# Attention rows and router logits turned by one TensorE product with an identity, stored by one DMA a step

## The chip, the core and the metric

The kernel runs on one core of a Trainium2 chip. Its engines work at the same time and wait for one another through semaphores: PE is TensorE (matrix products; PEld is its weight load), DVE is VectorE, ACT is ScalarE, POOL is GpSimd, and SP is the engine whose only work here is to issue DMAs. Matrix products read SBUF and write PSUM, which has eight banks of 128 partitions x 512 f32. The metric is the device time of one execution in microseconds (us); less is better. The kernel before took 461.04 us, the median of 3 runs (459.53 to 462.3).

## The reference

Two stages, of which the second takes the first one's result as its rows:

```python
# attention: q, k, v are (B, H, S, D) = (4, 8, 768, 64), blocks of 64 positions
for b in range(nb):
    qb, kb, vb = (q[:, :, sl], k[:, :, sl], v[:, :, sl])
    intra = np.einsum('bhic,bhjc->bhij', qb, kb) * Dmask[None]
    intra = np.einsum('bhij,bhjd->bhid', intra, vb)
    inter = np.einsum('bhid,bhde->bhie', qb * lam_pow[None], kv_state)
    out[:, :, sl] = intra + inter
    kv_state = lam_block[None, :, None, None] * kv_state + np.einsum('bhsd,bhse->bhde', kb * rev_pow[None], vb)
x = attn_out.transpose(0, 2, 1, 3).reshape(B * S, H * D)       # 3072 rows of 512
# router and experts: E = 8, w1 (8, 512, 1024), w2 (8, 1024, 512)
logits = x @ w_gate
expert_idx = np.argmax(logits, axis=1)
gate_w = softmax(logits)[arange, expert_idx]
for e in range(E):
    xe = x[expert_idx == e]
    out[expert_idx == e] = gate_w[..., None] * (np.maximum(xe @ w1[e], 0.0) @ w2[e])
```

## The kernel before, in words

**Attention.** It goes through 12 steps, six blocks of 128 positions (`n`) by two pairs of batch entries (`b`); one step takes 8 heads of two batch entries. In the loop of line 933 and after, `cur` is the step whose attention is finished now, `ahead` the next one, whose q and k are turned and scored already, and `last` the one before, whose rows leave now. The iterations are called i = 0 to 11 below. PE, DVE, ACT and SP do their work in the order in which the program writes it; POOL's larger work is chained one by one (`in_line`).

An iteration does, in this order on PE: `logits(last)` (four products against `gate`, line 361), `turn_ahead` (16 PE transposes of q and k, lines 242 and 257, into banks 0 to 3), the sum of the logits (`sum_logits`, line 368), the product of q with the running state (line 309, banks 6 and 7), the new state's product (`grow`, line 343, bank 4), scores times v (line 321, banks 6 and 7), the other half of line 309, every second iteration the ranks of the tokens within their experts (line 423, bank 5), and the scores of `ahead` (line 285, banks 0 to 3). DVE multiplies the scores by the decay mask (`mt`, line 291), which frees banks 0 to 3; ACT copies q and k out of PSUM (`qT`, `kT`, lines 244 and 259).

The attention's result stands in PSUM as features x tokens (`m.op`, banks 6 and 7). It is wanted twice: as it stands, for the router's logits (`to_sbuf`, an ACT copy `xT`), and as rows of tokens in DRAM (`xs`). DVE makes the rows by two 32x32-block transposes of 128 x 512 a step (`to_rows`, line 335); they leave a tile `x` in which a partition holds 32-wide pieces of many tokens, so `store_rows` (line 375) writes them by four DMAs a step with runs of 512 bytes. In half of the feature chunks the two heads of a pair stand in swapped order (`out_at`, `u ^ (hp & 1)`), and the rows keep that order; so `load_first` (line 191) loads the first weights of every expert pass by three DMAs, two of which swap halves of 64 rows.

Once a group of steps is complete, `choose` finds each token's expert on DVE, `weigh` its weight, `put` (line 423 and after) its slot, and POOL scatters slot entries to DRAM by indirect DMAs (line 436). SP issues, in one queue, the stores of `last` and the loads of step i + 3 (line 109: three DMAs of 512 KB in runs of 256 bytes), then at the loop's end the weights of the first pass.

**Experts.** After the loop the tokens of expert 0 come first, those of the early steps in a first part (`0a`), the others after it (`0b`), then the seven other experts, their products by a Strassen-like scheme of seven for eight (lines 692, 714 and 790). The rows are gathered from `xs` by POOL's indirect DMAs (line 520).

## Time and profile before

| What | Value |
|---|---|
| median of the runs | 461.04 us |
| the profiled execution, its own time | 459.43 us |
| its span, first to last instruction | 457.1 us |
| around the span | 2.3 us |
| busy PE, DVE, ACT, POOL | 423.9, 286.2, 140.6, 119.1 us |
| granted TensorE clock, mean | 0.981 of full |
| DMA, mean over the span | 209 GB/s, 138256 packets |
| end of the attention on PE | 139.4 us |
| first product of the experts | 142.6 us |

Rows of an engine's timeline read: start in us, duration, engine, line, operation, output<-input, shapes, how many in a row, and in brackets how long the engine was idle before and what ended it. `SPq` is SP's queue; a DMA row there is the time SP needed to hand the DMA over, not the transfer. A chain row "DMA a<-b" is the time from that hand-over to the data's landing. A row of a stretch gives its length, each engine's busy time with its instructions, the clock that PE was granted (1.00 is full), the share of the 16 DMA engines' time that packets took (it can pass 1, packets overlap), and what they moved in GB/s.

### The profile page before, as it was taken

Reading aid. Unit: us, or ns where it says so; the run is one execution under the profiler, and the core shown is the slowest. Engines: PE = TensorE matmul, PEld = TensorE weight load, DVE = VectorE, ACT = ScalarE, POOL = GpSimd, SP = SyncE. Lnnn points to the kernel's source line nnn. Section 1 sums busy time; section 2 is a strip of 40 time slices with the busy share of each in tenths; the row PEclk is TensorE's granted clock in tenths of the full one; section 3 lists DMA queues with packets and bytes.
Section 4 is the critical chain, followed back from the end, with each engine's and each line's share of the span. In section 5 each row is a group of like instructions: output and inputs, shape, how many; then the busy total and the mean of one; then the engine's idle time right before and its main releaser. Section 6 shows DMA issues by size and latency. Waiting matters only on the chain.

```text
span 457.1 us, 8958 instructions
## 1 busy us (share of the span) xinstructions
PE 423.9 (93%) x3527; PEld 387.9 (85%) x3527; DVE 286.2 (63%) x585; ACT 140.6 (31%) x298; POOL 119.1 (26%) x135
## 2 busy tenths in 40 slices
PE   3989897988889999898999999999999999999993
PEld 3877776867767749898999999999999999999873
DVE  3859494959476105798288568739938938948311
ACT  3344242433223111143134313413513512512511
POOL 5425353536143054005110320420230110010022
PEclk9999899999898999999999999999999999999998
DMA  9999998999998799977997997996995994613212
GB/s 177 235 213 211 154 213 175 201 169 198 187 260 141 229 235 259 325 189 193 359 225 214 371 217 183 364 266 172 335 294 123 331 275 97 227 67 70 69 66 71
DMA packets 138256, 95.53 MB, mean 209 GB/s; under 512 B 82787, under 2 KB 117223, under 8 KB 138205
## 3 DMA queue, kind: packets, MB, share of 16 engines
q1 hardware_dynamic: 130861, 80.76, 72.9%
q0 software_dynamic: 5264, 13.58, 10.4%
q10 hardware_dynamic: 2080, 0.52, 0.6%
q8 instruction: 30, 0.49, 0.5%
q14 instruction: 21, 0.17, 0.1%
HBM read 70.41 MB, written 24.65 MB: 208 GB/s over the span
## 4 chain that ended last, share of the span: by engine, by line
PE 70%; DMA 13%; DVE 8%; SPq 5%; issue 2%; ACT 1%; POOLq 0%; POOL 0%; DVEq 0%; ACTq 0%
PE p L692 26%; PE p L714 23%; DMA k_in<-in_k_dram 7%; PE ph L569 5%; PE po L818 5%; DMA qkv_in<-in_k_dram 4%; SPq L109 3%; PE p L790 3%; PE op L321 2%; PE tk L257 2%; PE po L734 2%; DVE ohc L402 1%; SPq L375 1%; DVE mt L291 1%; DMA ye<-yb 1%
## 5 line engine op out<-in xcount | busy, mean ns | idle before, releaser
L526 POOL DMA_INDIRECT out_dram<-o,list x21 | 22.1, 1054 | 166.9 <-ACT o L778 162.7
L714 PE MATMUL p<-hT,w2t 128*128 128x204 f32 (+3 forms) x288 | 49.9, 330 | 0.0
L714 PEld LDWEIGHTS p<-hT,w2t 128*128 128x128 f32 x288 | 48.2, 190 | 0.0
L702 ACT ACTIVATE hT<-hT 128x408 f32<-128x408 f32 (+4 forms) x56 | 29.4, 527 | 50.7 <-DVE hT L701 50.5
L692 PE MATMUL p<-xgT,w1t 128*128 128x204 f32 (+4 forms) x224 | 39.2, 328 | 0.0
L520 POOL DMA_INDIRECT xg<-xs,list x24 | 24.8, 1033 | 52.7 <-DMA list<-slots 31.1
L722 DVE TENSOR_TENSOR yT<-p,u_qsT 128x408 f32<-128x408 f32 (+3 forms) x18 | 10.2, 568 | 44.7 <-ACT u_qsT L608 29.2
L692 PEld LDWEIGHTS p<-xgT,w1t 128*128 128x128 f32 x224 | 37.1, 190 | 0.2 <-DVE xgT L546 0.2
L701 DVE TENSOR_TENSOR hT<-p,u_qsT 128x408 f32<-128x408 f32 (+4 forms) x42 | 23.4, 561 | 17.2 <-PE p L692 12.4
L291 DVE TENSOR_TENSOR mt<-sp,decay 128x512 f32<-128x512 f32 x48 | 29.8, 682 | 5.7 <-PE sp L285 5.7
L436 POOL DMA_INDIRECT slots<-entry,slot_i x24 | 23.6, 983 | 26.7 <-DVE slot_i L434 13.3
L285 PEld LDWEIGHTS sp<-qT,kT 64*128 64x128 f32 x384 | 23.5, 195 | 4.1 <-issue 2.0
L285 PE MATMUL sp<-qT,kT 64*128 64x128 f32 x384 | 25.9, 287 | 0.0
L330 ACT COPY xT<-op 128x512 f32<-128x512 f32 x24 | 12.9, 589 | 36.3 <-PE op L309 29.1
L595 ACT COPY u_qT<-p 128x408 f32<-128x408 f32 (+5 forms) x21 | 9.9, 473 | 45.2 <-PE p L692 39.4
L569 PE MATMUL ph<-xgT,w1t 128*128 128x256 f32 (+1 forms) x128 | 21.9, 331 | 0.5 <-DVE xgT L534 0.5
L692 PE MATMUL p<-xgT,s_k 128*128 128x204 f32 (+4 forms) x112 | 20.8, 329 | 1.4 <-ACT u_qsT L603 1.4
L569 PEld LDWEIGHTS ph<-xgT,w1t 128*128 128x128 f32 x128 | 19.5, 190 | 2.1 <-ACT xgT L532 0.6
L818 PE MATMUL po<-w2t,hT 128*128 128x512 f32 (+1 forms) x48 | 20.9, 592 | 0.0
L692 PE MATMUL p<-t_xT,s_q 128*128 128x204 f32 (+4 forms) x112 | 20.7, 328 | 0.0
L692 PE MATMUL p<-t_sd,w1t 128*128 128x204 f32 (+4 forms) x112 | 20.7, 328 | 0.0
L692 PE MATMUL p<-xgT,s_v 128*128 128x204 f32 (+4 forms) x112 | 20.7, 328 | 0.0
(189 smaller groups left out, 864.0 us busy)
## 6 DMA issues: line engine op xcount, KB each, us to landing
w2t<-in_moe_w_dram SPq DMA_DIRECT2D x8, 2048.0 KB
w1t<-in_moe_w_dram SPq DMA_DIRECT2D x8, 1024.0 KB
w1t<-in_moe_w_dram SPq DMA_DIRECT2D x16, 512.0 KB
xs<-x SPq DMA_DIRECT2D x48, 128.0 KB
xe<-xg SPq DMA_DIRECT2D x7, 512.0 KB
q_in<-in_q_dram SPq DMA_DIRECT2D x6, 512.0 KB
...
```

The lines of the kernel that those rows point to most:

```text
L109: queue.dma_start(out=t[:, b:b + per].rearrange("p b h d -> p (b h) d"), in_=src[b0 + b:b0 + b + per, :, n * C:(n + 1) * C, :].rearrange(" ...
L285: nc.tensor.matmul(sp[u][:, i, b, :], lhsT=m.kT[s][halves[u], i, b, :], rhs=m.qT[s][halves[u], i, b, :], start=(i == 0 and b == 0), stop=( ...
L291: nc.vector.tensor_mul(mt[:, u], sp[u], decay[:, u, s * HP // 2:(s + 1) * HP // 2].unsqueeze(2).to_broadcast(shp))
L436: in_line(nc.gpsimd.indirect_dma_start(out=slots, out_offset=bass.IndirectOffsetOnAxis(ap=slot_i[:, i:i + 1], axis=0), in_=entry[:, n, b, ...
L520: in_line(nc.gpsimd.indirect_dma_start(out=dst, out_offset=None, in_=xs[:rows, :], in_offset=bass.IndirectOffsetOnAxis(ap=idx, axis=0)))
L526: in_line(nc.gpsimd.indirect_dma_start(out=out, out_offset=bass.IndirectOffsetOnAxis(ap=idx, axis=0), in_=src, in_offset=None, bounds_chec ...
L569: nc.tensor.matmul(ph, lhsT=w1t[:, dc, fc * P:(fc + 1) * P], rhs=m.xgT[:, dc, 0, :m.h], start=(dc == 0), stop=(dc == DC - 1))
L692: nc.tensor.matmul(p[:, i, :], lhsT=lhs[:, dc, (c + i) * P:(c + i + 1) * P], rhs=rhs[:, dc, :], start=(first and i == 0 and dc == 0), stop ...
L701: nc.vector.tensor_add(outs[i][k], p, u)
L702: nc.scalar.activation(outs[i][k], outs[i][k], ACT.Relu)
L714: nc.tensor.matmul(p[:, i, :], lhsT=rhs[:, fc, i * P:(i + 1) * P], rhs=lhs[:, fc, :], start=(first and i == 0 and fc == 0), stop=(end and ...
L818: nc.tensor.matmul(po[part], lhsT=m.hT[:, fc, t * P:t * P + w], rhs=w2t[:, fc, :], start=(i < k), stop=(i >= FC - k), skip_group_check=True)
```

## The change

`back` takes the place of `gate` and `sel`: for each of the two pairs of feature chunks it holds two matrices, a 128x128 identity with 8 columns of the router's weights beside it, the second with the identity's halves swapped. `rows(m, b, lg)` multiplies each 128-feature chunk of `xT` by such a matrix. Two chunks share one bank: the 8 logit columns of both fall on the same place and are added there, and the 2 x 128 columns at their sides are the chunk's tokens as rows, in the reference's feature order. ACT then copies, for each of the four banks 4 to 7, the 8 logit columns and the 256 row columns to SBUF. `to_rows`, `logits` and `sum_logits` are gone; `choose` begins with one addition of the two partial logits; `store_rows` is one DMA; `load_first` is one DMA; `leave` (with the store) comes at the head of an iteration, and `rank` takes bank 5 when it needs it.

```diff
--- before.py
+++ after.py
@@ -120,15 +120,16 @@
     make_identity(nc, ident)
 
 
-    gate = const.tile([P, DC, Q], F32, name="gate")
-    nc.gpsimd.memset(gate, 0.0)
-    sel = const.tile([P, E], F32, name="sel")
-    nc.vector.reduce_sum(sel, ident.rearrange("p (c e) -> p e c", c=DC)[:, :E], axis=AX.X)
-    by_chunk = moe_w_gate.rearrange("(c j h p) e -> j h p c e", c=DC // 2, j=2, h=2)
-    for j in range(2):
-        for h in range(2):
-            nc.gpsimd.dma_start(out=gate[h * D:(h + 1) * D].rearrange(
-                "p (c j) e -> p j c e", j=2)[:, j, :, :E], in_=by_chunk[j, h ^ j])
+    W = P + E
+    back = const.tile([P, DC // 2, 2 * W], F32, name="back")
+    for c in range(DC // 2):
+        nc.gpsimd.tensor_copy(back[:, c, :P], ident)
+        nc.gpsimd.tensor_copy(back[:, c, P + 2 * E:W + E + D], ident[:, D:])
+        nc.gpsimd.tensor_copy(back[:, c, W + E + D:], ident[:, :D])
+    by_chunk = moe_w_gate.rearrange("(c j u d) e -> j u d c e", c=DC // 2, j=2, u=2)
+    for j, u in itertools.product(range(2), range(2)):
+        nc.gpsimd.dma_start(out=back[(u ^ j) * D:((u ^ j) + 1) * D, :, P + j * E:P + (j + 1) * E],
+                            in_=by_chunk[j, u])
 
     before = const.tile([P, P], BF16, name="before")
     make_upper_triangular(nc, before, val=1.0, diag=False)
@@ -185,10 +186,7 @@
 
     def load_first(e):
         w1t = wpool.tile([P, DC, F], F32, tag="w1", name="w1t")
-        src = pick(w1_r, e)
-        for j, h in ((0, slice(0, P)), (1, slice(0, D)), (1, slice(D, P))):
-            fr = slice(0, P) if j == 0 else slice(D - h.start, P + D - h.stop)
-            nc.sync.dma_start(out=w1t[h, j::2], in_=src[fr, j::2])
+        nc.sync.dma_start(out=w1t, in_=pick(w1_r, e))
         return w1t
 
     def load_second(e):
@@ -210,7 +208,6 @@
         return ps.tile(shape, F32, tag=f"bank{i}", name=name)
 
 
-    five = bank(5, [P, 4 * C], "five")
 
     st = once.tile([P, B, HP, D], F32, tag="h2", name="st")
     zeros = work.tile([P, P], F32, tag="x", name="zeros", bufs=4)
@@ -325,15 +322,10 @@
                 skip_group_check=True)
 
     def to_sbuf(m):
-        m.xT = work.tile([P, 2, DC, C], F32, tag="xT", name="xT", bufs=1)
         for b in range(2):
-            nc.scalar.copy(m.xT[:, b], m.op[b])
-
-    def to_rows(m):
-        m.x = row_pair("x")
-        for b in range(2):
-            nc.vector.transpose(m.x[:, b].rearrange("p (t d f) -> p t d f", d=DC, f=Q),
-                                m.op[b].rearrange("p d (t f) -> p t d f", f=Q))
+            xT = work.tile([P, DC, C], F32, tag="xT", name="xT")
+            nc.scalar.copy(xT, m.op[b])
+            m.xT.append(xT)
 
     def grow(m):
 
@@ -355,29 +347,34 @@
             else:
                 nc.vector.tensor_add(to, m.cp, m.sd)
 
-    def logits(m):
-        lt = five[:, :2 * C].rearrange("p (b c) -> p b c", b=2)
-        for c in range(DC):
-            nc.tensor.matmul(lt[c * Q:(c + 1) * Q], lhsT=gate[:, c, :], rhs=m.xT[:, :, c, :],
-                             start=True, stop=True, skip_group_check=True)
-        m.lt = small.tile([P, 2, C], F32, tag="lt", name="lt", bufs=1)
-        nc.scalar.copy(m.lt, lt)
-
-    def sum_logits(m, lg):
-        for b in range(2):
-            nc.tensor.matmul(lg[:, b], lhsT=m.lt[:, b, :], rhs=sel, start=(b == 0), stop=(b == 1),
-                             skip_group_check=True)
+    def rows(m, b, lg):
+
+        if b == 0:
+            m.x = row_pair("x")
+        x = m.x[:, b]
+        tx = [bank(4 + 2 * b + c, [P, 2, W], f"tx{c}") for c in range(DC // 2)]
+        for c, t in enumerate(tx):
+            flat = t.rearrange("p j w -> p (j w)")
+            nc.tensor.matmul(flat[:, :W], lhsT=m.xT[b][:, 2 * c, :], rhs=back[:, c, :W],
+                                 start=True, stop=False, skip_group_check=True)
+            nc.tensor.matmul(flat[:, P:P + W], lhsT=m.xT[b][:, 2 * c + 1, :],
+                                 rhs=back[:, c, W:], start=False, stop=True,
+                                 skip_group_check=True)
+        for c, t in enumerate(tx):
+            nc.scalar.copy(lg[:, c, :], t[:, 0, P:])
+
+            nc.scalar.copy(x.rearrange("p (a d f) -> p d a f", a=P // Q, d=DC)[:, 2 * c:2 * c + 2],
+                           t[:, :, :P].rearrange("p d (a f) -> p d a f", f=Q))
 
     def store_rows(m):
         r0 = 1 + (m.n * B + m.b) * C
-        to = xs[r0:r0 + 2 * C, :].rearrange("(b t f) (a g) -> a f (b t) g", b=2, f=Q, a=P // Q)
-        for a in range(P // Q):
-            nc.sync.dma_start(out=to[a], in_=m.x[a * Q:(a + 1) * Q].rearrange(
-                "f b (t g) -> f (b t) g", g=P))
+        nc.sync.dma_start(out=xs[r0:r0 + 2 * C, :].rearrange("(b p) f -> p b f", p=C), in_=m.x)
 
     def choose(n, bs, lg):
         nb = len(bs)
         shp = [P, nb, E]
+        parts, lg = lg, small.tile(shp, F32, tag="lg_sum", name="lg_sum")
+        nc.vector.tensor_add(lg, parts[:, :, 0], parts[:, :, 1])
         mx = small.tile([P, nb, 1], F32, tag="mx", name="mx")
         nc.vector.reduce_max(mx[:, :, 0], lg, axis=AX.X)
         sh = small.tile(shp, F32, tag="sh", name="sh")
@@ -418,7 +415,7 @@
 
         nb = len(bs)
         shp = list(oh.shape)
-        rank = five[:, 3 * C:3 * C + shp[1] * E].rearrange("p (b e) -> p b e", e=E)
+        rank = bank(5, shp, "rank")
         for lhs, rhs in ((before, oh), (ones, ohc[:, :shp[1]])):
             nc.tensor.matmul(rank, lhsT=lhs, rhs=rhs, start=(lhs is before),
                              stop=(lhs is ones))
@@ -652,7 +649,7 @@
     def token_sums(m):
         b = [[m.xgT[:, j * DH:(j + 1) * DH, k, m.off[k]:m.off[k] + m.h] for k in range(2)] for j in range(2)]
         t1, t2, t4 = (work.tile([P, DH, m.h], F32, tag=t, name=f"t_{t}", bufs=n)
-                      for t, n in (("sd", 2), ("xT", 1), ("kd", 2)))
+                      for t, n in (("sd", 2), ("xT", 2), ("kd", 2)))
 
         m.b = right_sums(b, t1, t2, b[0][1], t4, nc.vector.tensor_sub)
 
@@ -861,14 +858,14 @@
         return m
 
     def leave(m):
-        n, bs = group_of[m.n, m.b]
-        i = bs.index(m.b)
-        if i == 0:
-            lgs[0] = small.tile([P, len(bs), E], F32, tag="lg", name="lg")
-        lg = five[:, 2 * C:2 * C + 2 * E].rearrange("p (b e) -> p b e", b=2)
-        sum_logits(m, lg)
-        nc.scalar.copy(lgs[0][:, i:i + 2], lg)
-        if i + 2 == len(bs):
+        for b in range(2):
+            n, bs = group_of[m.n, m.b + b]
+            i = bs.index(m.b + b)
+            if i == 0:
+                lgs[0] = small.tile([P, len(bs), DC // 2, E], F32, tag="lg", name="lg")
+            rows(m, b, lgs[0][:, i])
+        store_rows(m)
+        if i == len(bs) - 1:
             return choose(n, bs, lgs[0])
 
     had = const.tile([P, 1], F32, name="had")
@@ -942,9 +939,7 @@
                         turn_q(ahead, s)
                         turn_k(ahead, s)
 
-            if last:
-                logits(last)
-                store_rows(last)
+            new = leave(last) if last else None
             if i + AT_ONCE < len(order):
                 load(i + AT_ONCE)
             if i == len(order) - 3:
@@ -953,7 +948,6 @@
                 turn_ahead()
             else:
                 later_decays()
-            new = leave(last) if last else None
             if new:
                 weigh(*new)
             attend_states(cur, 0)
@@ -981,12 +975,10 @@
             if ahead:
                 for s in range(2):
                     score(ahead, s)
-            to_rows(cur)
             last, cur = cur, ahead
-        store_rows(last)
         w2t = load_second(0)
         turn_rows(passes[0], (0, 1), lambda shp: ffn.tile(shp, F32, tag="xgT", name="xgT", bufs=1),
-                  1, lambda t: t or logits(last))
+                  1)
         new = leave(last)
         weigh(*new)
         zero, rest = passes[0], make_pass(0, EARLY, CAPS[0] - EARLY, 1, "0b")
```

**PE, from the end of one step's scores to the end of the next step's turned q and k** (the iteration i = 3; `sp` are scores, `tq` and `tk` turned q and k, `five` the logits' bank, `tx` the new rows' banks). The numbers tell tiles of one name apart. Before:

```order
L285 MATMUL sp1_634<-qT_509,kT_518 128x128
L361 MATMUL five_157<-xT_617,gate_93 32x256 x4
L242 MATMUL tq_665<-ident_88,q_in_356 128x128 x4
L257 MATMUL tk_674<-ident_88,k_in_357 128x128 x4
L242 MATMUL tq_681<-ident_88,q_in_356 128x128 x4
L257 MATMUL tk_690<-ident_88,k_in_357 128x128 x4
L368 MATMUL five_157<-sel_95,lt_653 128x8 x2
L309 MATMUL op0_701<-qsT_495,st_158 64x128
```

With the change:

```order
L358 MATMUL tx0_668<-back_93,xT_636 128x136
L360 MATMUL tx0_668<-back_93,xT_636 128x136
L358 MATMUL tx1_669<-back_93,xT_636 128x136
L360 MATMUL tx1_669<-back_93,xT_636 128x136
L358 MATMUL tx0_678<-back_93,xT_638 128x136
L360 MATMUL tx0_678<-back_93,xT_638 128x136
L358 MATMUL tx1_679<-back_93,xT_638 128x136
L360 MATMUL tx1_679<-back_93,xT_638 128x136
L239 MATMUL tq_695<-ident_88,q_in_369 128x128 x4
L254 MATMUL tk_704<-ident_88,k_in_370 128x128 x4
L239 MATMUL tq_711<-ident_88,q_in_369 128x128 x4
L254 MATMUL tk_720<-ident_88,k_in_370 128x128 x4
```

Eight products of 136 columns stand where four of 256 stood, and the two small products that stood behind the turns are gone.

**DVE, from the end of one step's masks to the next state, in an iteration with a choice** (the iteration i = 4; `mt` are masked scores, `qsT` the decayed q that reads the turned q's bank, `mx` to `ohc` the choice). Before:

```order
L291 TENSOR_TENSOR mt<-sp_777,decay 128x512
L335 STREAM_TRANSPOSE x<-op_701 128x512
L335 STREAM_TRANSPOSE x<-op_702 128x512
L248 TENSOR_TENSOR qsT<-tq,qdec 128x512 x2
L382 TENSOR_REDUCE mx<-lg 128x4
L384 TENSOR_TENSOR sh<-lg,mx 128x32
L387 SCALAR_TENSOR_TENSOR key<-sh,rev 128x32
L391 TENSOR_REDUCE pick<-key 128x4
L397 TENSOR_TENSOR oh<-key,pick 128x32
L400 COPY ohc<-ohc 128x8
L402 TENSOR_TENSOR ohc<-ohc,oh 128x8 x4
L412 TENSOR_REDUCE sm<-ex 128x4
```

With the change:

```order
L288 TENSOR_TENSOR mt<-sp_804,decay 128x512
L377 TENSOR_TENSOR lg_sum<-lg 128x32
L379 TENSOR_REDUCE mx<-lg_sum 128x4
L381 TENSOR_TENSOR sh<-lg_sum,mx 128x32
L384 SCALAR_TENSOR_TENSOR key<-sh,rev 128x32
L388 TENSOR_REDUCE pick<-key 128x4
L394 TENSOR_TENSOR oh<-key,pick 128x32
L397 COPY ohc<-ohc 128x8
L399 TENSOR_TENSOR ohc<-ohc,oh 128x8 x4
L245 TENSOR_TENSOR qsT<-tq,qdec 128x512 x2
L409 TENSOR_REDUCE sm<-ex 128x4
```

The two transposes are gone, and the choice, which stood behind `qsT`, stands ahead of it.

**SP, from a store inside the loop to the loads behind it, and the loop's end** (`xs<-x` is a store of rows, `w1t` and `w2t` are the first pass's weights). Before:

```order
L375 DMA xs<-x 32x8x128 x4
L109 DMA q_in<-in_q_dram 128x16x64
L109 DMA k_in<-in_k_dram 128x16x64
L109 DMA v_in<-in_v_dram 128x16x64
L375 DMA xs<-x 32x8x128 x4
L191 DMA w1t<-in_moe_w_dram 128x2x1024
L191 DMA w1t<-in_moe_w_dram 64x2x1024 x2
L375 DMA xs<-x 32x8x128 x12
L196 DMA w2t<-in_moe_w_dram 128x8x512
```

With the change:

```order
L371 DMA xs<-x 128x2x512
L109 DMA q_in<-in_q_dram 128x16x64
L109 DMA k_in<-in_k_dram 128x16x64
L109 DMA v_in<-in_v_dram 128x16x64
L371 DMA xs<-x 128x2x512
L189 DMA w1t<-in_moe_w_dram 128x4x1024
L371 DMA xs<-x 128x2x512 x2
L194 DMA w2t<-in_moe_w_dram 128x8x512
L371 DMA xs<-x 128x2x512
```

Four stores a step are one; at the end the second weights go ahead of the last step's store, where they stood behind it.

## The prediction, made before the changed kernel was run

> **What bounds the kernel now.** I first read the attention step by step: one row for a stretch of each iteration, cut where its first logits product starts (the columns are named in the first line). Iterations 5 to 8, 10 and 11:
>
> ```profile
> core 0: us, PE busy (x) PEld busy (x) DVE busy (x) ACT busy (x) POOL busy (x), PEclk, DMA share, GB/s
> 64.33:73.89 9.56, 9.56 (x158) 7.88 (x156) 6.16 (x11) 4.01 (x9) 6.97 (x7) 1.00 0.92 170
> 73.89:87.15 13.26, 10.80 (x160) 9.38 (x158) 9.95 (x26) 4.34 (x10) 3.04 (x3) 0.87 0.97 206
> 87.15:96.70 9.55, 9.55 (x158) 7.88 (x156) 6.15 (x11) 4.00 (x9) 6.96 (x7) 1.00 1.00 152
> 96.70:109.40 12.70, 9.94 (x161) 7.99 (x159) 10.13 (x29) 3.95 (x10) 3.06 (x3) 1.00 0.95 205
> ...
> 119.36:131.52 12.16, 9.92 (x128) 8.37 (x126) 7.83 (x26) 4.14 (x10) 3.49 (x4) 0.86 1.01 236
> 131.52:139.43 7.91, 6.50 (x81) 4.74 (x79) 4.67 (x16) 2.05 (x6) 3.18 (x4) 0.79 1.10 222
> ```
>
> Every second iteration takes about 9.6 us with PE never idle; the others take 12.2 to 13.3 us, idle for 2.2 to 2.8 us. The DMA engines are at 0.92 to 1.10 in all of them. The chain of work that ended last says what the long ones wait for:
>
> ```profile
> 24.58 0.63 PE tk L257 x4
> ...
> 43.77 10.49 DMA k_in<-in_k_dram
> ...
> 112.70 9.94 DMA k_in<-in_k_dram
> ...
> 122.77 1.08 PE tk L257 x4
> ```
>
> The turn of k waits for k to land, about 10 us after SP handed the load over. Whether SP was late or the transfers are slow stands in SP's timeline:
>
> ```profile
> 26.53 2.34 SPq L109 DMA_DIRECT2D qkv_in<-in_v_dram  x1
> 28.98 4.45 SPq L375 DMA_DIRECT2D xs<-x  x4
> 33.48 0.50 SPq L109 DMA_DIRECT2D q_in<-in_q_dram  x1
> ...
> 74.02 4.86 SPq L375 DMA_DIRECT2D xs<-x  x4
> ```
>
> SP is never free: a hand-over that takes 0.50 us when there is room takes 2.34 us behind other loads, so it is the queue that is full. It is behind PE, too: the store of iteration 5, which began at 64.33, goes out at 74.02, and its rows were made long before. The attention is paced by DMA, with PE close behind (9.55 us of work in a mean of 11.3, from 64.33 to 109.40). After 142.6 us the experts follow, nearly all PE, and I found nothing of the change there but three DMAs becoming one.
>
> **The change part by part. The store**, on the path. Rates in stretches of loads (16 to 24), of stores almost alone (33 to 35, 123 to 125) and of weights in runs of 2 KB (185 to 189), same columns:
>
> ```profile
> 16.00:24.00 8.00, 6.06 (x76) 4.83 (x72) 7.41 (x13) 3.99 (x8) 1.70 (x2) 1.00 1.05 238
> 33.00:35.00 2.00, 2.00 (x33) 1.81 (x33) 2.00 (x4) 1.72 (x5) 0.00 (x0) 1.00 0.91 213
> 123.00:125.00 2.00, 2.00 (x11) 2.00 (x11) 0.00 (x0) 0.79 (x2) 0.00 (x0) 0.50 1.06 254
> 185.00:189.00 4.00, 4.00 (x29) 3.80 (x28) 3.12 (x4) 0.61 (x2) 0.00 (x0) 1.00 1.05 384
> ```
>
> A step's store is 4 x 128 KB = 524 KB. At 213 GB/s it holds the engines for 2.46 us, at 384 GB/s for 1.37 us: 1.1 us saved a step. Lower end: from 254 GB/s, 2.06 - 1.37 = 0.7 us. Upper end: the four hand-overs follow each other at 0.5 us, so that three fewer may save 1.5 us where SP, not the engines, sets the pace:
>
> ```profile
> 42.13 0.47 SPq L375
> 42.65 0.47 SPq L375
> ```
>
> (The distance of such rows, 0.52 us, is what one hand-over costs.)
>
> I take 1.1 us, since the 213 GB/s stretch is the one inside the loop. [...]
>
> Eight stores stand in SP's queue ahead of k of step 11, which ends the last wait (122.77): 8 x 1.1 = 8.8 us (5.6 to 12). By DMA alone that turn of k starts at 114.0 (110.8 to 117.2). The store now waits for ACT and not for DVE, and the loads stand behind it on SP; its rows are ready 2.5 us after the iteration's start (below), where SP comes to it 9.7 us after: no wait, and none as long as SP gains less than 7 us on PE.
>
> **PE.** Removed and added stand in PE's timeline; the last row is a product of the new one's very shape, 128x128 weights by 136 columns:
>
> ```profile
> 17.25 0.60 PE L257 MATMUL tk<-ident,qkv_in 128*128 128x128 f32 x4
> 17.69 0.60 PE L242 MATMUL tq<-ident,qkv_in 128*128 128x128 f32 x4
> ...
> 64.33 0.64 PE L361 MATMUL five<-xT,gate 128*32 128x256 f32 x8
> 64.90 0.66 PE L242 MATMUL tq<-ident,q_in 128*128 128x128 f32 x4
> 65.47 0.66 PE L257 MATMUL tk<-ident,k_in 128*128 128x128 f32 x4
> ...
> 67.16 0.51 PE L368 MATMUL five<-sel,lt 128*128 128x8 f32 x4
> 67.60 0.95 PE L309 MATMUL op<-qsT,st 64*64 64x128 f32 x16
> ...
> 171.91 7.65 PE L569 MATMUL ph<-xgT,w1t 128*128 128x136 f32 x64 [0.54 <-DVE xgT L534]
> ```
>
> The logits take 64.90 - 64.33 = 0.57, their sum 67.60 - 67.16 = 0.44: 1.01 us go. A product is two instructions in the trace; 7.65 / 64 = 0.12 us each, so 8 products are 16 x 0.12 = 1.91 us. Net +0.90, and a full step is 9.55 + 0.90 = 10.45 us. Against it: turns follow each other at 0.57 us here but at 0.44 us at 17.25, where they wait for no mask to free their bank. Now 1.9 us of products stand ahead of them, the masks are done, and four groups may save 4 x 0.13 = 0.5; the 0.95 us of the row at 67.60, which waited for the DVE transpose to leave its bank, may fall to 0.67 as in its other half. So 9.65 to 10.45 a step. From the turn of k in iteration 1 (24.58, ahead of any store) to that of iteration 10 are nine steps: PE can be there at 111.4 at the earliest, at 118.6 at 10.45.
>
> The four groups, the product of line 309 and the two logits rows are in every full step. The two bounds cross, so neither term alone is the answer. I take 115.0 for that turn, 1 us behind the DMA's 114.0, for waits that remain where both are near: **-7.8 us**.
>
> **ACT** gets eight copies a step and loses two:
>
> ```profile
> L364 ACT COPY lt<-five 128x256 f32<-128x256 f32 x12 | 4.5, 373 | 22.5 <-PE five L361 20.3 <-issue 1.6 <-ACT xgT L532 0.6
> L870 ACT COPY lg<-five 128x16 f32<-128x16 f32 x12 | 2.2, 182 | 0.9 <-PE five L368 0.9
> ```
>
> 4 x (0.373 + 0.182) - 0.555 = +1.7 us on 4.0 of 9.55: room enough. Behind them on ACT are the copies of q and k, and the banks 6 and 7, which line 309 wants. PE delivers a bank each 0.48 us, a pair of copies takes 0.55, so ACT ends some 0.6 us after PE's last new product, under turns of 1.8 us: hidden. In iteration 11 there are no turns; there the 1.91 + 0.6 = 2.5 us stand bare, where 133.98 - 131.52 = 2.46 us stood (logits, their sum, and waits): 0.
>
> ```profile
> 133.98 0.40 PE L309 MATMUL op<-qsT,st 64*64 64x128 f32 x2 [0.67 <-DVE x L335]
> ...
> 142.60 1.99 PE L569 MATMUL ph<-xgT,w1t 128*128 128x256 f32 x8
> ```
>
> **DVE** loses 1.3 us a step, and in every second one has the choice ahead of `qsT`. The choice took up to 4.3 us, because its four sums collided with POOL:
>
> ```profile
> 58.01 0.19 DVE L382 TENSOR_REDUCE mx<-lg 128x4 f32<-128x32 f32 x1 [0.27 <-ACT lg L870]
> 59.21 3.17 DVE L402 TENSOR_TENSOR ohc<-ohc,oh 128x8 bf16<-128x8 bf16 x4
> ...
> 59.13 2.04 POOL L268 TENSOR_TENSOR kd<-k_in,kdec 128x512 f32<-128x512 f32 x2 [9.39 <-PE cp L343]
> ...
> 71.91 2.06 PE L285 MATMUL sp<-qT,kT 64*128 64x128 f32 x32
> ```
>
> Counted from the end of the scores, the logits are in SBUF at 1.9 + 0.3, the slow choice ends at 6.5, `qsT` frees bank 0 at 7.2, and the next scores, the last 2.06 us of a step, want it at 9.65 - 2.06 = 7.6: hidden, by 0.4 us. Without that cover each of five choices would cost what it is late, and PE would wait there. POOL's product then starts after the choice rather than in it, so it should be short.
>
> **The rest.** POOL builds `back` by six copies at the start, under 4 us of idle time; if they took longer, the first `kd` would be late by the rest, once:
>
> ```profile
> 11.34 1.04 POOL L268 TENSOR_TENSOR kd<-qkv_in,kdec 128x512 f32<-128x512 f32 x1 [3.97 <-DVE kdec L171]
> ```
>
> The last store goes behind 2 MB of weights (5.5 us at 384 GB/s), but these are handed over in iteration 11, before its rows exist. The first weights of a pass are the same bytes in one hand-over in place of three, off the chain: 0. Late next is the early gather, whose chain from the slots of iteration 8 keeps its length:
>
> ```profile
> 137.24 0.62 ACT L552 COPY xo<-xg 128x512 f32<-128x512 f32 x1 [1.23 <-DMA xg<-xs,list_0a]
> 139.52 1.07 ACT L330 COPY xT<-op 128x512 f32<-128x512 f32 x2 [1.67 <-PE op L309]
> ```
>
> It has 1.67 us to spare ahead of ACT's last `xT`; three shorter iterations take about 2: cost 0 to 1, say +0.3. Behind the attention, the eight products (1.9) and the eight turns of gathered rows (some 1.2 at 0.6 for four) take the place of the 3.2 us from 139.43 to 142.60: 0. Against that, the sum at 122.77 to 131.52 loses its 0.5 us.
>
> Sum: -7.8 + 0.3 - 0.5 = -8.0 us. The profiled execution's own time is 459.43 (span 457.1 and 2.3 around it), so 451.4; it lies 1.6 under the median of the runs, and from that 461.04 - 8.0 = **453.0 us**. The forecast's own range is 448 to 457.
>
> **The rivals.**
>
> *PE becomes the bound at 10.45 us a step*, the turns no denser than now: turn of k at 118.6, -4 us, 457 (455 to 459). For it: DVE's masks still take 2.5 us. Against it: they end before the new products do.
>
> *The store was never the price*: DMA takes as long with it in 2 KB, s between 0 and 0.2, 459.5 to 461. For it: the slow stretches (152 and 170 GB/s) are those of POOL's slot scatters, which stay. Against it: the rates above, and the hand-overs. [...]
>
> *ACT holds banks 6 and 7*, the slower end: if a pair of new copies, strided into 32-wide runs, takes 1.2 us and not 0.55, ACT ends 0.5 + 4 x 1.2 = 5.3 us after the scores, PE wants the banks at 1.9 + 1.8 = 3.7, and a step is 9.65 + 1.6 = 11.3 to 12.1 us: nine of them, 24.58 + 105 = 130, +7 us, 468 (463 to 472). It decides from 0.85 us a pair, and is slower than before from about 1.1. Against it: the copy `xo` above is permuted in the same runs and takes 0.62 us for 512 columns, where a plain one takes 0.59.
>
> **How the numbers follow.** Forecast 0.63, PE bound 0.15, store not the price 0.12, ACT 0.10. What a measurement can tell here from no change is about 0.5%, 2.3 us. Faster by more: the forecast and most of the PE case, 0.76; within: 0.14; slower: 0.10. The range from 447.5 to 460.0 holds the first two and half of the third.
>
> **What would show it.** Right: long and short iterations even out near 10 us; the chain in the attention is PE's rather than "DMA k_in"; one SP row of about 0.5 us a store; stretches of stores near 300 GB/s; attention over near 131.5. Wrong: iterations still alternate with waits for k (store not the price), or line 309's successor waits for ACT's row copies in every step (ACT), or all iterations are 10.5 us and more with PE never idle (PE).

## The result, and the profile after

The changed kernel took 444.95 us (median of four runs, 443.4 to 449.14) beside 460.64 for the kernel before: ratio 0.967, interval 0.960 to 0.974. Faster, as forecast, but by 15.7 us where 8 were forecast. Measured again beside the kernel before, on two other chips, the same kernel gave 0.982 (0.974 to 0.989) and 0.976 (0.967 to 0.985), 9.5 and 10.0 us by the medians. So two questions are open here: where the first measurement found twice the forecast, and what takes a part of it back elsewhere.

The profiled execution of the first measurement took 445.17 us (span 443.3, 1.9 around it), 14.3 less than the one before. Its iterations 5 to 8, 10 and 11, in the columns of the prediction's first fence:

```profile
core 0: us, PE busy (x) PEld busy (x) DVE busy (x) ACT busy (x) POOL busy (x), PEclk, DMA share, GB/s
60.03:69.84 9.81, 9.81 (x163) 9.01 (x161) 4.80 (x9) 4.93 (x15) 6.72 (x7) 1.00 0.98 160
69.84:79.95 10.11, 10.11 (x165) 9.19 (x163) 7.42 (x25) 5.06 (x16) 3.22 (x4) 1.00 1.04 228
79.95:93.23 13.28, 11.17 (x163) 10.37 (x161) 5.40 (x10) 4.93 (x15) 6.73 (x7) 0.90 1.13 182
93.23:103.49 10.26, 10.26 (x163) 9.42 (x163) 6.68 (x28) 5.03 (x16) 3.15 (x4) 0.97 1.05 229
...
113.30:122.60 9.30, 9.24 (x132) 8.16 (x130) 6.74 (x25) 5.03 (x16) 1.46 (x2) 1.00 0.99 332
122.60:128.58 5.98, 5.88 (x85) 4.73 (x83) 3.56 (x15) 3.36 (x12) 4.46 (x6) 1.00 0.85 225
```

Long and short iterations are gone: 9.8 to 10.3 us with PE never idle, where 9.6 alternated with 12.2 to 13.3. One iteration (79.95) still takes 13.3; PE waited there 2.11 us for nothing that the profile shows, and its clock came down to 0.90. SP has one row a store (`L371`), and it is still the full queue that sets their length:

```profile
57.30 3.45 SPq L371 DMA_DIRECT2D xs<-x  x1
60.86 0.40 SPq L109 DMA_DIRECT2D qkv_in<-in_q_dram  x1
61.32 2.54 SPq L109 DMA_DIRECT2D qkv_in<-in_k_dram  x1
63.91 3.64 SPq L109 DMA_DIRECT2D qkv_in<-in_v_dram  x1
67.65 4.96 SPq L371 DMA_DIRECT2D xs<-x  x1
```

The difference of the two traces in us, cut at the events that the prediction used (all from PE's timeline):

| Stretch | before | after | change | forecast |
|---|---|---|---|---|
| start to the turn of k in iteration 10 | 122.77 | 115.69 | -7.1 | -7.8 |
| from there to the first product of the experts | 19.83 | 15.65 | -4.2 | -0.2 |
| from there to pass 1 (first expert after expert 0) | 44.38 | 44.68 | +0.3 | 0 |
| pass 1 | 43.70 | 40.29 | -3.4 | 0 |
| rest of the span | 226.4 | 227.0 | +0.6 | 0 |
| around the span | 2.3 | 1.9 | -0.5 | 0 |

So the attention's loop came out near the forecast. What was missed lies in two places: the end of the attention (from the turn of k in iteration 10 on) and pass 1.

**The end of the attention.** In what is left of iteration 10 after that turn, before:

```profile
122.77 1.08 PE L257 MATMUL tk<-ident,k_in 128*128 128x128 f32 x4 [2.18 <-DMA k_in<-in_k_dram]
123.65 1.06 PE L242 MATMUL tq<-ident,q_in 128*128 128x128 f32 x4
124.50 1.06 PE L257 MATMUL tk<-ident,k_in 128*128 128x128 f32 x4
125.35 0.74 PE L368 MATMUL five<-sel,lt 128*128 128x8 f32 x4
126.02 0.67 PE L309 MATMUL op<-qsT,st 64*64 64x128 f32 x16
```

and after:

```profile
115.69 0.60 PE L254 MATMUL tk<-ident,k_in 128*128 128x128 f32 x4
...
117.10 0.67 PE L306 MATMUL op<-qsT,st 64*64 64x128 f32 x16
```

From the turn of k to line 309 (306 after) it takes 1.41 us where it took 3.25. The sum of the logits, which is gone, had 0.67 of these 1.84 us; the other 1.17 are the three groups of turns, which ran at a clock of 0.50 behind the wait for k (the row 123.00 to 125.00 in the prediction) and run at 1.00 now. That is all that iteration 10 gained behind the turn.

PE's timeline of iteration 11, before:

```profile
132.70 0.61 PE L368 MATMUL five<-sel,lt 128*128 128x8 f32 x4 [0.54 <-ACT lt L364]
...
135.17 3.18 PE L321 MATMUL op<-mt,v_in 128*64 128x128 f32 x32
138.29 1.13 PE L309 MATMUL op<-qsT,st 64*64 64x128 f32 x16
```

and after, the last two products again:

```profile
125.85 2.13 PE L318 MATMUL op<-mt,v_in 128*64 128x128 f32 x32
127.91 0.67 PE L306 MATMUL op<-qsT,st 64*64 64x128 f32 x16
```

They are the same instructions and take 2.80 us where they took 4.31. The granted clock goes with it; two stretches of before, 1 us each:

```profile
133.00:134.00 1.00, 0.33 (x4) 0.27 (x3) 1.00 (x3) 0.17 (x1) 0.70 (x2) 1.00 1.05 225
...
137.00:138.00 1.00, 1.00 (x14) 0.95 (x10) 0.00 (x0) 0.62 (x1) 0.00 (x0) 0.50 1.33 273
```

PE idles for a part of 132 to 135 us (0.33 us busy from 133 to 134), and the clock is at half from 136 to 139, behind the waits. After, PE is busy nearly throughout (0.93 us or more in each us) and the clock stays at 1.00. The waits need not have this price: before_store_one, below, has the same three and its line 321 takes 2.13 us. So that these waits caused the half clock is inferred from the order of events, not shown.

Together, the 4.2 us are 1.8 in iteration 10, 1.9 in iteration 11 (1.5 of them these two products) and 0.4 between the attention and the first product of the experts.

**Pass 1** is that of the first expert after expert 0. Before, PE waited twice in it, on ACT's copies, which waited for DVE, which waited for the gathered rows of pass 1 (`xb`):

```profile
185.81 2.10 DVE L546 STREAM_TRANSPOSE xgT<-xb 128x896 f32<-128x896 f32 x2 [6.54 <-DMA xb<-xe]
...
194.41 1.70 PE L692 MATMUL p<-xgT,s_k 128*128 128x212 f32 x8 [1.43 <-ACT u_qsT L603]
216.07 3.13 PE L714 MATMUL p<-s_h,t_k 128*128 128x212 f32 x16 [1.33 <-ACT u_qT L595]
```

After, the rows are there 7.9 us ahead of the pass (176.02), and DVE waits for nothing:

```profile
168.09 2.10 DVE L543 STREAM_TRANSPOSE xgT<-xb 128x896 f32<-128x896 f32 x2
```

### The profile page after: what moved, and what is told of

Its sections match the earlier page's. It is cut to its first block, busy times and chain, and to the rows that moved or that the text cites. A ratio compares the mean times of both kernels' runs of the same rounds, so it can differ in the third digit from the quotient of the medians.

```text
span 443.3 us, 9039 instructions
## 1 busy us (share of the span) xinstructions
PE 424.9 (96%) x3575; PEld 397.9 (90%) x3575; DVE 265.7 (60%) x567; ACT 152.7 (34%) x370; POOL 120.5 (27%) x140
## 4 chain that ended last, share of the span: by engine, by line
PE 90%; SPq 3%; DMA 2%; DVE 1%; ACT 1%; issue 1%; POOLq 0%; POOL 0%; DVEq 0%
PE p L689 29%; PE p L711 25%; PE sp L282 5%; PE po L815 5%; PE ph L566 4%; PE op L318 4%; SPq L109 3%; PE p L787 3%; PE op L306 3%; PE tx L358 2%; PE cp L335 2%; DMA qkv_in<-in_k_dram 2%; PE tx L360 2%; PE tk L254 2%; PE tq L239 2%; PE po L731 2%
## 5 line engine op out<-in xcount | busy, mean ns | idle before, releaser
L719 DVE TENSOR_TENSOR yT<-p,u_qsT 128x408 f32<-128x408 f32 (+3 forms) x18 | 10.2, 568 | 44.7 <-ACT u_qsT L605 29.2
L282 PEld LDWEIGHTS sp<-qT,kT 64*128 64x128 f32 x384 | 24.4, 200 | 3.7 <-issue 2.9
L689 PE MATMUL p<-t_sd,w1t 128*128 128x204 f32 (+4 forms) x112 | 20.7, 328 | 0.0
L689 PE MATMUL p<-xgT,s_k 128*128 128x204 f32 (+4 forms) x112 | 20.7, 328 | 0.0
L689 PE MATMUL p<-t_xT,s_q 128*128 128x204 f32 (+4 forms) x112 | 20.7, 328 | 0.0
L689 PE MATMUL p<-t_kd,w1t 128*128 128x204 f32 (+4 forms) x112 | 20.7, 328 | 0.0
## 6 DMA issues: line engine op xcount, KB each, us to landing
w2t<-in_moe_w_dram SPq DMA_DIRECT2D x8, 2048.0 KB, 11.1
```

The lines of the kernel that those rows point to most:

```text
L282: nc.tensor.matmul(sp[u][:, i, b, :], lhsT=m.kT[s][halves[u], i, b, :], rhs=m.qT[s][halves[u], i, b, :], start=(i == 0 and b == 0), stop=( ...
L689: nc.tensor.matmul(p[:, i, :], lhsT=lhs[:, dc, (c + i) * P:(c + i + 1) * P], rhs=rhs[:, dc, :], start=(first and i == 0 and dc == 0), stop ...
```

## The experiments

Each stands beside runs of the kernel before on its own chip, "before, beside it"; the first four and the last two ran on chip 5, the next four on chip 0, then four on chip 11 and four on chip 6. Times are medians. "Turn" is the turn of k in iteration 10 and "first product" that of the experts, both in us from the start of the one profiled execution.

| Kernel | us | before, beside it | ratio (interval) | turn | first product |
|---|---|---|---|---|---|
| before_w1_one | 455.59 | 463.82 | 0.984 (0.976 to 0.992) | 123.56 | 143.49 |
| before_store_one | 453.73 | 463.82 | 0.985 (0.975 to 0.995) | 111.98 | 133.33 |
| after_w1_halves | 450.84 (446.1 to 458.5) | 463.82 | - | 112.42 | 132.06 |
| after_w1_three | 447.93 | 463.82 | 0.967 (0.959 to 0.975) | 118.47 | 134.11 |
| after_store_512 | 451.96 | 463.41 | 0.975 (0.968 to 0.982) | 120.71 | 140.40 |
| after_store_32p | 451.33 | 463.41 | 0.974 (0.967 to 0.980) | 118.42 | 138.07 |
| after_turns_first | 463.42 | 463.41 | 1.000 (0.996 to 1.003) | 128.10 | 150.29 |
| before_both | 454.54 | 463.41 | 0.981 (0.973 to 0.988) | 118.08 | 142.71 |
| after_again | 453.22 | 462.71 | 0.982 (0.974 to 0.989) | 117.42 | 139.39 |
| after_loads_first | 453.98 | 462.71 | 0.981 (0.975 to 0.988) | 118.19 | 140.78 |
| after_turns_loads | 462.57 | 462.71 | 1.000 (0.996 to 1.003) | 128.36 | 148.51 |
| before_both_again | 454.29 | 462.71 | 0.981 (0.974 to 0.988) | 120.76 | 146.81 |
| after_third | 451.88 | 461.86 | 0.976 (0.967 to 0.985) | 117.01 | 140.11 |
| before_store_one_b | 456.75 | 461.86 | 0.989 (0.979 to 0.999) | 116.03 | 140.17 |
| after_store_512_b | 452.94 | 461.86 | 0.981 (0.972 to 0.990) | 118.54 | 136.62 |
| after_plain_slots | 441.13 | 461.86 | 0.954 (0.945 to 0.963) | 112.64 | 128.29 |
| before_again | 462.76 | 463.62 | 0.999 (0.996 to 1.002) | 126.57 | 146.02 |
| before_plain_slots | 448.35 | 463.62 | 0.968 (0.961 to 0.975) | 117.10 | 135.76 |

### The weights' load

```diff
# before_w1_one
-        for j, h in ((0, slice(0, P)), (1, slice(0, D)), (1, slice(D, P))):
-            ...
-            nc.sync.dma_start(out=w1t[h, j::2], in_=src[fr, j::2])
+        nc.sync.dma_start(out=w1t, in_=pick(w1_r, e))
# after_w1_halves
+        for j, h in ((0, slice(0, P)), (1, slice(0, D)), (1, slice(D, P))):
+            nc.sync.dma_start(out=w1t[h, j::2], in_=src[h, j::2])
# after_w1_three
+        for c in (slice(0, 4, 2), slice(1, 2), slice(3, 4)):
+            nc.sync.dma_start(out=w1t[:, c], in_=src[:, c])
```

> The kernel before, with only the first weights of a pass in one plain load. (It leaves out the swap of halves in two of the four feature chunks, so the experts' first products meet rows and weights in a different order; the work is the same.) Theory H (the two loads that write 64 partitions each run at about half the rate, so the queue is late in pass 1): pass 1 loses its two waits of 1.3 to 1.4 us and some of its slow products, 43.7 to about 40.2 us; the time falls by 3 to 4 us, to 457, and the attention stays at 139.4. Rival Q (pass 1 gained because the attention's smaller store traffic left the queues empty): 0, 460.6, pass 1 stays at 43.7.

> The changed kernel, with the first weights of a pass in three loads again, of 128, 64 and 64 partitions as in the kernel before, rows plain. (It leaves the swap out, which the changed rows do not need.) Theory H: the two half loads run at about 215 GB/s, pass 1 goes from 40.1 back toward 43.7, the time to 448 to 449. Rival Q: no difference, 445, pass 1 at 40.1.

> The changed kernel, with the first weights of a pass in three loads of 128 partitions each (two feature chunks, one, one): as many hand-overs as before, but full partitions. Theory H (64 partitions are what is slow): 445, pass 1 at 40.1, rates near 380 GB/s. Rival N (the number of hand-overs is what costs): 448 to 449, as with the halves.

The rates, in the profile's stretches. Before, a part of the load's first DMA (128 partitions), then the two of 64:

```profile
127.60:128.80 1.20, 1.20 (x25) 1.03 (x22) 1.03 (x7) 0.00 (x0) 0.00 (x0) 1.00 1.01 389
128.90:133.60 4.70, 3.87 (x62) 2.98 (x62) 3.61 (x9) 1.62 (x4) 2.21 (x3) 1.00 1.06 219
```

after_w1_halves, the same:

```profile
148.80:149.90 1.10, 1.10 (x4) 0.51 (x3) 0.00 (x0) 0.00 (x0) 0.71 (x1) 1.00 1.03 421
150.00:154.50 4.50, 4.50 (x12) 2.08 (x11) 0.75 (x1) 0.00 (x0) 3.28 (x5) 1.00 1.05 228
```

after_w1_three, 1.5 of the 2 MB that its three DMAs move:

```profile
150.80:154.40 3.60, 3.60 (x10) 1.67 (x9) 0.00 (x0) 0.00 (x0) 2.62 (x3) 1.00 1.02 419
```

The DMAs of 64 partitions move at half the rate of those of 128 (219 and 228 against 389 to 421 GB/s), and the number of hand-overs changes the rate by nothing that shows. The 1 MB of the halves takes 4.7 us where at some 405 GB/s, the middle of 389 and 421, it would take 2.6 (an estimate), 2.1 us a load, in the queue in which the rows of pass 1 stand.

But theory H, by which the halves also caused the waits of pass 1, holds in part only. In before_w1_one the two waits of pass 1 are gone and the stretch from its start to the end of the span falls from 270.1 to 266.7 us, while the loop is as before. In after_w1_halves they do not come back: from pass 1's start the span has 267.4 us, as in the changed kernel (267.3), because the rows of pass 1, though later, still land 4.4 us ahead of it (172.29 against 176.71). And in before_store_one, with the slow halves, they are gone too (267.3). Either the quicker load or the quicker attention is enough to bring the rows in time; the 3.4 us are earned once. By the medians before_w1_one gained more than that, 8.2 us. Its trace and that of before_again, from the same chip, lie 7.0 us apart, of which 2.8 are from pass 1 on; the rest lies in waits of the loop and in the first eight products of the experts (2.00 us against 3.67, at half the clock), and whether the load has a part in it is not shown. (Two of the four runs of after_w1_halves took 455 and 458 us, and no profile shows why.)

### The store

```diff
# before_store_one, before_store_one_b (before_both, before_both_again: and the one load above)
-        for a in range(P // Q):
-            ...
+        nc.sync.dma_start(out=xs[r0:r0 + 2 * C, :].rearrange("(b p) f -> p b f", p=C), in_=m.x)
# after_store_512, after_store_512_b (to: the rows of xs as in the one store)
+        for a in range(4):
+            nc.sync.dma_start(out=to[:, :, a * P:(a + 1) * P], in_=m.x[:, :, a * P:(a + 1) * P])
# after_store_32p
+        for a in range(4):
+            nc.sync.dma_start(out=to[a * Q:(a + 1) * Q], in_=m.x[a * Q:(a + 1) * Q])
```

> The kernel before, with only the store of a step as one DMA in runs of 2 KB straight from the transposed tile. (It leaves out the reordering, so the rows in DRAM hold the pieces of other tokens; the work is the same.) Theory S (the store alone held the attention back): the waits for k go, a full step comes to 9.6 to 9.8 us, the attention ends at 127 to 130 in place of 139.4. Under theory H the waits in pass 1 stay (43.7) and the total falls by 9.5 to 12, to 449 to 451. Under rival Q pass 1 falls to 40.2 as well: 445 to 447. Rival P (the store is a small part, the denser order on PE gave the gain): the attention still alternates and ends at 135 or later, 456 or more.

> The kernel before, with both DMA changes and nothing on PE, ACT or DVE: one store of 2 KB runs straight from the transposed tile and one plain load of the first weights. (It leaves out the reordering of the rows and the swap of the weights' halves; the work is the same.) If the whole gain is the DMAs': first product of the experts near 131 to 133, pass 1 without waits, 445 to 448, and the rows' products on PE bring nothing but the right order. If PE's new order has a part of the gain: 450 or more.

> The changed kernel, with a step's store in four DMAs again, each of 128 partitions and a quarter of the features, so in runs of 512 bytes; PE, ACT and DVE unchanged. Theory R (the run length sets the DMA's pace): the loads of the loop go back from one in 10.3 us to one in 11.2 or more, long and short iterations come back with waits for k, the first product of the experts goes from 131 to 140 or later, the time to 453 to 458. Rival O (the order on PE and the rows on ACT gave the gain, the store is hidden): no change, 445 to 448.

> The changed kernel, with a step's store in four DMAs of 32 partitions each, runs of 2 KB kept. Theory R (only the run length counts): as the changed kernel, 445 to 448. Rival T (few partitions slow a DMA down, as they did the weights at 64): stores at half their rate or less, 2 us and more a step, first product of the experts at 140 or later, 453 or more. Rival U (the number of hand-overs holds SP): 3 x 0.5 = 1.5 us a step only if SP is not waiting for the queue anyway, at most 5 us in all, 447 to 451.

> The kernel before with the one store (rows not reordered), a second time, beside the changed kernel on one chip. If the store alone is the gain of the attention: turn of k in iteration 10 within 2 us of the changed kernel's, pass 1 without waits, total within 3 us of it. If the products' place on PE brings more than they cost: 4 us and more behind it.

> The changed kernel with the store in four DMAs with runs of 512 bytes, a second time, beside the changed kernel on one chip. Theory R (runs of 512 bytes cost DMA 0.5 us and more a step, and DMA decides): turn of k in iteration 10 at least 3 us behind the changed kernel's, total 3 to 6 us more. If its 452 us of the first time was the chip's: within 1.5 us of the changed kernel.

> The kernel before with both DMA changes once more (rows not reordered, halves not swapped). In its first run ACT stood still for 7.3 us and DVE for 3.1 us in iteration 11 with nothing in the profile that released them, and the first product of the experts came at 142.7 in place of 132. If that was chance: first product at 132 to 134, 446 to 449. If it belongs to the program: 142 again, 453 to 456.

The one store alone takes the waits for k out of the old loop: turn of k at 111.98 and 116.03, where the two traces of the kernel before have 122.77 and 126.57. This is theory S. Its end comes out worse, though: from that turn to the first product 21.4 and 24.1 us, and on the one chip where both ran it is 4.9 us behind the changed kernel, outside the 3 us of "the store alone". The two traces do not put that to the products' place on PE, as the expectation would: before_store_one_b has its turn 1.0 us earlier than after_third and its first product at the same time. What it loses comes behind:

```profile
140.17 3.78 PE L566 MATMUL ph<-xgT,w1t 128*128 128x256 f32 x8
```

and in after_third, on the same chip:

```profile
140.11 1.89 PE L566 MATMUL ph<-xgT,w1t 128*128 128x256 f32 x8
```

The first eight products of the experts ran at a clock of 0.50, behind a wait of 4.39 us for ACT's last `xT`; they and what follows them up to pass 1 make 2.3 of the 3.1 us between the two spans. What the place on PE is worth is shown by other runs, below.

Adding the one load (before_both) brought nothing further in either run that the intervals could tell (ratios 0.981 and 0.981 against 0.985 and 0.989); its first product came at 142.7 and 146.8, after ACT and DVE had stood still in iteration 11. From the waits of the first (us in total, times, longest):

```profile
ACT lt L361 <- remote: 7.3, 1, 7.3
```

It did so twice, so it is no single accident, and the forecast of 446 to 449 for a repeat fell (the profiled execution of that repeat took 459.98 us, its other three 452.4 to 455.3). What held ACT, the profile does not show. The changed kernel stands still at the same place on chips 11 and 6, beside POOL's scatters (below), so this does not come from the old order of the work.

Theory R is not borne out in its size. The 512-byte store beside the changed kernel on one chip: turn of k 1.5 us later, 452.94 against 451.88, which the intervals do not part. The loads of steps 4 to 11 do come 10.9 us apart there, beside 10.2 in after_third, but little of that reaches the turn of k. The 452 of the first such run was the chip's or the execution's. after_store_32p had no changed kernel beside it and the same stops as described below; it stays inconclusive, except that its stores, where little else disturbs them, take 2.3 to 2.7 us as one store of the changed kernel does. The old store had both, 32 partitions and runs of 512 bytes; no run puts both back into the changed kernel, so which of the two made it slow is not shown.

### The place on PE and on SP

```diff
# after_turns_first (after_turns_loads: load and load_first stay at the head)
-            new = leave(last) if last else None
-            ...                            (load, load_first)
             if i:
                 turn_ahead()
             else:
                 later_decays()
+            new = leave(last) if last else None
+            ...                            (load, load_first)
# after_loads_first
-            new = leave(last) if last else None
             ...                            (load, load_first)
+            new = leave(last) if last else None
```

> The changed kernel, with the rows' products behind the turns of q and k as the logits' sum was, store and loads of SP in the same order behind them. The prediction's step on PE (the new products in front let the turns follow each other at 0.44 us and line 309's first half run in 0.67): turns 0.57 apart again, line 309 waits for ACT's copies of the rows, a step 9.82 + 0.5 + 0.3 or more = 10.6 us and over, first product at 137 to 141, the time 450 to 456. Rival (the place does not matter, since DMA's 10.3 us a step pace it anyway): 445 to 448.

> As the kernel with the turns first, but SP hands over the loads ahead of the rows' store, so that no load waits for ACT's copies: this parts the order on PE from the order on SP. If the order on PE costs the 16 us (turns wait for the masks, line 309 for ACT's last copy of the rows): steps stay at 11.6, DMA idles, 461 to 464. If the loads behind the late store cost it: steps of 10 to 10.5, 447 to 452.

> The changed kernel with the load of step i + 3 ahead of the store in SP's queue, all else as it is. If the DMA still decides in the loop (10.3 us a step against PE's 9.8): loads come up to 2 us earlier, PE never waits, all iterations at 9.8, the turn of k in iteration 10 at 113 to 114, the time 1 to 3 us under the changed kernel's, unless the gather of the early rows then holds the first product at 131 to 132, which would give 0. If PE decides: 0.

With the same DMAs and the same products, only behind the turns, the kernel is exactly as slow as the kernel before. PE in one iteration of after_turns_first:

```profile
92.07 0.66 PE L239 MATMUL tq<-ident,qkv_in 128*128 128x128 f32 x4 [0.46 <-DVE mt L288]
92.67 0.66 PE L254 MATMUL tk<-ident,qkv_in 128*128 128x128 f32 x4
...
96.44 0.43 PE L306 MATMUL op<-qsT,st 64*64 64x128 f32 x2
97.88 0.66 PE L306 MATMUL op<-qsT,st 64*64 64x128 f32 x14 [1.01 <-ACT x L366]
```

The turns wait 0.46 us for the masks and then follow each other at 0.60 us, and line 306 waits 1.01 us for ACT's last copy of the rows: some 1.8 us more in a step of 11.6. Loads handed over early do not help (after_turns_loads, 462.57, although its loads come 9.8 us apart), so it is the place of the rows' work on PE (and of ACT's copies and DVE's choice, which move with it), not SP's queue. In the changed kernel's place, turns at 0.44 us and line 306 without a wait, the same work fits into 9.8. Loads ahead of the store bring nothing there (453.98 beside 453.22): in the changed kernel PE decides in the loop, and DMA is just quick enough.

### The same kernel again, and the scatters

```diff
# after_again, after_third, before_again: no edit.  after_plain_slots, before_plain_slots:
-            in_line(nc.gpsimd.indirect_dma_start(
-                out=slots, out_offset=bass.IndirectOffsetOnAxis(ap=slot_i[:, i:i + 1], axis=0),
-                in_=entry[:, n, b, :], in_offset=None), "put")
+            in_line(nc.gpsimd.dma_start(
+                out=slots[E * R - N + (n * B + b) * P:][:P], in_=entry[:, n, b, :]), "put")
```

> The changed kernel once more, unaltered, beside the next three on one chip. From the table of the runs so far: turn of k in iteration 10 at 115.5 to 118.5, 15.6 us from there to the first product of the experts where neither the gathered rows nor a late block of instructions holds PE, pass 1 in 40.1, 443 to 449 in all. One iteration of 13 us where all others take 10 is expected again if it is chance (a wait of PE for nothing that the profile shows), in another iteration than 7; in iteration 7 again if it belongs to the program.

> The changed kernel a third time, as the measure for the three beside it on this chip. If the chip decides: either as at first (even steps of 9.8 to 10.1, no moment in which PE, ACT and DVE all begin nothing for 0.6 us and more behind POOL's scatters, first product of the experts at 131 to 134, 443 to 449) or as in its second run (stops of 0.7 to 0.9 us in every second iteration and of several us in iteration 11, first product at 139, 453 to 455). If it is chance from run to run: anything between, with a spread of 8 us over the rounds.

> The kernel before, unaltered, once more with a profile, so that a trace of it exists from a second chip. If the stops behind POOL's scatters are of the scatters and the chip, whichever kernel: stops of 0.6 us and more in every second iteration and several us in iteration 11 here too, the first product of the experts at 144 to 148, hidden in part by the waits for k. If they come only with the changed kernel: waits for k as in its first trace, first product at 142 to 143, pass 1 in 43.7.

> The changed kernel with POOL's scatters of the slots' entries replaced by plain DMAs of the same 128 entries to fixed rows. (It leaves the placing of tokens out, so the lists are empty and all gathers fetch one row; the attention's work is the same.) If the scatters stop the other engines: no stops behind them, odd iterations at 9.8, and where the changed kernel has its first product at 139, here 131 to 133. If they have nothing to do with it: the same stops as in the changed kernel beside it. Where the changed kernel has no stops: no difference in the attention.

> The kernel before with POOL's scatters replaced by plain DMAs of the same 128 entries, as was done to the changed kernel (tokens are not placed, all gathers fetch one row), so that the change can be weighed without the scatters: 441.1 is the changed kernel's time so. If the store in runs of 512 bytes paces the attention by itself: waits for k stay, the turn of k in iteration 10 at 119 to 122 against 112.6, total 453 to 457, the change worth 12 to 16 us. If the scatters slowed the loads and that made the waits: turn of k at 112 to 114.5, total 445 to 449, the change worth 4 to 8 us.

POOL scatters slot entries in every second iteration, four DMAs of 128 entries each. In after_again these iterations take 11.1 us and the last one 13.2, at a clock of 0.74 and with the DMA engines mostly idle:

```profile
72.41:82.36 9.95, 9.95 (x164) 9.11 (x162) 7.25 (x25) 5.03 (x16) 3.21 (x4) 1.00 1.05 250
82.36:93.45 11.09, 10.26 (x162) 9.20 (x160) 4.79 (x9) 5.13 (x15) 6.73 (x7) 1.00 0.90 192
...
124.33:137.53 13.20, 9.43 (x92) 7.68 (x91) 4.23 (x19) 3.95 (x14) 4.88 (x6) 0.74 0.40 116
```

The long ones are those in which POOL scatters (6.73 us busy). 0.24 us after the last of the four scatters, at 87.22, there is a stop: nothing begins on PE, ACT or DVE for 0.70 us, and PE's row says that it waited for nothing known:

```profile
87.92 0.88 PE L335 MATMUL cp<-qkv_in,kd 128*64 128x64 f32 x23 [0.71 <-issue]
```

after_third has the same stops, and its chain of waits names the one in iteration 11:

```profile
123.04 6.05 another core or an unknown queue
```

On the same chip after_plain_slots, whose entries go out by plain DMAs, has none of them:

```profile
70.20:80.16 9.96, 9.96 (x165) 9.12 (x163) 7.26 (x25) 5.03 (x16) 4.73 (x7) 1.00 1.14 257
80.16:89.97 9.81, 9.81 (x163) 9.01 (x161) 4.80 (x9) 4.92 (x15) 3.44 (x4) 1.00 1.02 228
...
119.56:126.44 6.88, 6.78 (x93) 5.63 (x91) 4.16 (x19) 3.97 (x14) 1.07 (x2) 1.00 0.49 135
```

Steps of 9.8 and 9.96, the first product at 128.29 in place of 140.11, 441.13 us in place of 451.88: more than the 6 us by which the repeats fall short of the first measurement. So the stops behind the four scatters are the scatters'; by what way they come about is not shown. For the long stop of iteration 11 the run parts less, since with empty lists POOL's two gathers moved too, from 123 to 107 us.

Whether the stops come goes with the chip in every trace. In all eleven from chips 0, 11 and 6 with scatters there is such a stop of 0.6 to 0.9 us, beginning within 0.4 us of the end of the last scatter, in each of four iterations. In the two of the first measurement and the five of chip 5 there is none, though these have the same scatters. The kernel does not decide it: before_store_one has none on chip 5 and before_store_one_b has all four on chip 6. That is the answer to the second question above, as far as it goes; what differs between the chips is open, and there is no trace of the unaltered kernel before from a chip with stops.

Without scatters both kernels can be weighed with no stops, though not on one chip: 448.35 on chip 5 against 441.13 on chip 6. The change is worth 7.2 us so, or 5.5 if each is taken from the kernel before beside it (15.3 and 20.7 us under it). In before_plain_slots the waits for k stay; four of them:

```profile
65.25 0.63 PE L257 MATMUL tk<-ident,k_in 128*128 128x128 f32 x4 [2.64 <-DMA k_in<-in_k_dram]
75.50 0.63 PE L257 MATMUL tk<-ident,qkv_in 128*128 128x128 f32 x4 [1.24 <-DMA qkv_in<-in_k_dram]
...
107.22 0.63 PE L257 MATMUL tk<-ident,k_in 128*128 128x128 f32 x4 [1.28 <-DMA k_in<-in_k_dram]
117.10 0.63 PE L257 MATMUL tk<-ident,k_in 128*128 128x128 f32 x4 [0.87 <-DMA k_in<-in_k_dram]
```

The waits that stay are what the first branch said, the total and the worth of the change lie in the second (445 to 449, 4 to 8 us), and the turn of k at 117.10 lies between the two. So scatters and store shared the waits. Of the 6.6 us between the spans (446.3 and 439.7), 4.5 are in the loop (turn of k 117.10 and 112.64) and 3.0 at the attention's end (18.66 and 15.65); from the first product on the changed kernel is 0.9 slower, and pass 1 gives it nothing.

## Why the prediction was right and wrong

- **DMA paces the old loop, the store is a part of it: right; the size of the store's term is in part luck.** The first packets of the loads of steps 4 and 11 lie 10.26 us a step apart after and 11.27 before: 1.0 us saved a step, 1.1 forecast. The old loop loses its waits by the store alone (before_store_one). But the argument by rates, which set a store against a read of weights, overstated the store itself: where little disturbs it, its packets take 2.3 to 2.7 us after and 2.8 to 3.2 before, about 0.5 us apart and not 1.1. Where the other half of the 1.0 us comes from no run shows; without scatters (before_plain_slots) the old loop's loads come 10.4 us apart with the old store.
- **PE's step of 9.65 to 10.45: right, at its lower end** (9.81 and 10.1; the eight new products took 1.96 us, 1.91 forecast). The denser turns and the freed line 306 were needed: with the order reversed a step is 11.6 us, and the whole gain is gone. That is the rival "PE becomes the bound", harsher than priced, one line away.
- **The turn of k at 115.0: right,** 115.69, and 117.0 to 117.4 in the repeats.
- **ACT, DVE, POOL hidden: right.** A pair of ACT's new copies took 0.56 us, as forecast. The choice on DVE is hidden in the first measurement, by the little that was forecast: in after_w1_three and after_store_32p the turn of k in iteration 10 waited 0.98 and 0.71 us for it.
- **"End of the attention: 0" and "i=10's rest: -0.5": failed,** -4.2 together. The step set iteration 11's bare 2.5 us of products against the 2.46 us of logits, sum and waits that they replace, and stopped there. It left out that PE's clock was 0.86 and 0.79 in the rows it had itself quoted, so that the products behind a wait had a price too: with the waits gone, the same products of iteration 11 took 2.80 us instead of 4.31, and in iteration 10 the turns behind the wait for k took 1.17 us less beside the logits' sum (0.67), the only part that it counted there. A part of this is luck, since the same waits in before_store_one left the clock at 1.00.
- **"The first weights are the same bytes in one hand-over, off the chain: 0": failed** in the first measurement, by the 3.4 us of pass 1. Bytes were counted and not partitions, and "off the chain" was read from one trace without asking how late the rows behind that load were: in before they came 1.2 us ahead of the pass, with DVE and ACT still to follow. Since the quicker attention alone also removes those waits, the term is not the load's own; it is lead time, which either part buys.
- **The signs:** the loop's chain went to PE, and two stretches of stores ran at 290 and 297 GB/s, as named. But SP's row of a store in the loop took 1.7 to 5.0 us and not 0.5: the queue stays full.
- **The rival "store not the price"** rested on the slow stretches being the scatters'. It had a point: without scatters the kernel before falls by about 15 us. But the waits for k stay, and the one store alone removes them.
- **453.0 itself** was met on two chips (453.22, 451.88) and missed on the first, and where it was met that was luck: pass 1 gained where nothing was forecast (in after_third 267.2 us from its start, 270.1 before), and iteration 11 gave about 7 us back to the stops (13.2 and 13.4 us for 6.0).
